# Half blocks of 78 destinations instead of 72, and extra keys added in small chunks between tiles, in a gather and scatter-add kernel

## The chip, the core and the metric

The kernel runs on one core of a Trainium2 chip. The metric is the device time of one execution in microseconds (us), the median of several runs. Engine names are those of the profile: PE is TensorE (matmul), PEld its weight loads, DVE is VectorE, ACT is ScalarE, POOL is GpSimd, SP is SyncE.

## The reference

The task is one GraphSAGE layer with mean aggregation. 800,000 edges go between 12,500 nodes, with random source and destination, and each node has 64 features.

```python
N, deg, D = 12500, 64, 64
E = N * deg
src = randint(0, N, E);  dst = randint(0, N, E)

def reference(x, src, dst, deg_inv, w_self, w_neigh):
    N = x.shape[0]
    nsum = _segment_sum(x[src], dst, N)
    h_neigh = nsum * deg_inv[:, None]
    return x @ w_self + h_neigh @ w_neigh
```

So for each edge a row of x is fetched by source and added into a sum by destination. The two small products and the scaling follow at the end.

## The kernel before

**Buckets.** Sources are cut into 98 blocks (NB) of 128. Destinations are cut into blocks of two halves with HN = 72 destinations each, which gives 87 destination blocks (NDB). A pair of a destination block and a source block is a bucket: 87 x 98 = 8526 buckets (NBID). Each bucket has 128 slots for edges, 64 (H) for each half of its destinations. An edge is one 32-bit key that holds destination block, source block, half, source and destination in it. Buckets are stored as rows of keys: part 0 has 128 rows of 41 buckets each, part 1 has 128 rows of 27 (KPRS).

**First half of the time.** `make_keys` builds the keys. `sort_runs` sorts the 6250 keys of each partition on DVE (lines 230 to 245). `find_rows` counts where each row starts in each of the 128 sorted runs, `gather_runs` (L473, POOL, one indirect DMA per run) brings the pieces of all runs to the partition of their row, and `merge_runs` (L284, L296, L313, L328, DVE) merges them. The lengths that a merge keeps at each level are LENS. `find_buckets` (part 0, on ACT, L610) counts where each bucket's middle lies in its row; `gather_buckets` (L633, POOL) fetches a window of 2 x SIDE = 2 x (64 + EXT) keys around each middle; `decode_buckets` splits the windows, four buckets at a time (L680 to L685 on DVE, L690 and L694 on ACT, a transpose on PE at L700, a copy on ACT at L701), into the 64 + 64 slots and writes the slots' sources to memory (sl). Part 1 goes the same way later, with `find_and_gather` counting on DVE (L612).

**Extra keys.** A half of a bucket with more than 64 edges has keys left over. They lie in the EXT keys at either end of the window. `beyond` (L717, L720) makes them stand out as positive numbers, `pieces` (L745) takes the 8 largest of each of PCS = 8 interleaved pieces of a row, and `leftovers` compacts them: the rows go to memory and come back 16 rows (GRP) to a partition (L756, L757), the 8 largest of 16 pieces are taken again, and the result goes to memory (lt) and back to turn it. This gives 8 chunks per part, each of at most 128 extra keys from 16 rows. `wide` is a row of numbers that the place of a key within its destinations is compared with.

**Second half of the time.** `nodes` walks the buckets in tiles of 8. For each tile `one_hots` has loaded the slots' sources (slb, SP) and built on DVE two one-hot matrices per 28 buckets: ohs (L799, 128 x 3584, which source) and ohd (L802, 128 x 28 x 72, which destination). `gather` multiplies ohs with the block of x on PE (L827, one matmul of 128 columns per bucket) into PSUM (ct), and ACT (L837), or from tile SHARE = 540 on in some tiles DVE (L835), copies the result to xg. `sums` multiplies xg with ohd into acc (L883, two matmuls of 72 columns per bucket, one for each half of the slots, which use 64 rows of the array each). OCT = 7 destination blocks make an octet; its sums stand in two PSUM tiles. When an octet is done, the extra keys of all its chunks are added: their rows of x were fetched (L864, POOL, from 300 buckets ahead on), one-hot matrices of 504 columns are built (L876, DVE), and matmuls of 504 columns add them (L888). Then g is copied out (L891, L893), and `finish` multiplies with the weights (L951), scales (L957), adds (L958) and writes (L959, issued on POOL).

**What runs beside the tiles.** `sums_and_merge` drives everything of part 1 from the loop over tiles: for each tile it grants the merge of part 1 a budget of 280 ns (`t += 280`); when that merge has ended it makes one step of `find_and_gather` in every second tile, then one step of `decode_buckets` per tile, and then `leftovers(1)`. Part 1 must be decoded before its first bucket is due. A scheduler that works on a modelled time orders the instructions of each engine, except where a manual schedule is given (the sort and the first merges).

Of the kernel before, what the change touches and what calls it, by code (L numbers as in the profile page):

```python
# [46 lines left out]
CHK = 128 // GRP  # L47
BIGBITS = 0x7E000000
# [10 lines left out]
BEHIND = 6  # L59
NEARLY = 36  # L60
LAG = 4
OCT = 7

# [276 lines left out]
class Kernel:  # L340
    def __init__(self, tc, ctx, ins, outs):
        self.tc, self.nc, self.ctx = tc, tc.nc, ctx
        self.I, self.O = ins, outs
        self.keep = ctx.enter_context(tc.tile_pool(name="keep", bufs=1))
        self.dram = ctx.enter_context(tc.tile_pool(name="dram", bufs=1, space=DRAM))
        self.d1 = self.dram.tile([128, PITCH1], F32, name="d1")
        self.sl = self.dram.tile([NCOL, 128], BF, name="sl")
        self.xt = self.dram.tile([NB * 128, 128], FH, name="xt")
        self.tops = [self.dram.tile([128, PCS * 9], F32, name=f"tops{p}") for p in range(2)]
        self.lt = [self.dram.tile([CHK, 128], F32, name=f"lt{p}") for p in range(2)]  # L350
        self.d2 = [self.dram.tile([128, PITCH2[p]], F32, name=f"d2_{p}") for p in range(2)]

    def setup(self):
# [15 lines left out]
        for p in range(2):  # L369
# [6 lines left out]
                       allow_small_or_imprecise_dtypes=True)  # L376
        self.wide = keep.tile([128, OCT * HN], FH, name="wide")
        nc.gpsimd.iota(self.wide, pattern=[[1, OCT * HN]], base=0, channel_multiplier=0,
                       allow_small_or_imprecise_dtypes=True)
# [287 lines left out]
    def decode_buckets(self, part, v, vp, mps):  # L667
# [56 lines left out]
        for step in range(per * (len(groups) - 1) + plan[0][0] + 1):  # L724
            for wait, what in plan:
                g, odd = divmod(step - wait, per)
                if not odd and 0 <= g < len(groups):
                    held[g] = what(*groups[g], held.get(g))
            yield min(step // 2 * 4, kpr - 1)
            if part == 0 and step == per * (NEARLY // 4 - 1):  # L730
                beyond(0, NEARLY, 0, PCS - 2)()
                yield -1
        if part == 0:
            beyond(NEARLY, kpr - NEARLY, PCS - 2, 2)()
        else:
            pick = beyond(0, kpr, 0, PCS)
            yield kpr
            pick()
# [7 lines left out]

    def leftovers(self, part):


        nc = self.nc  # L750
        pool = self.fin
        n = PCS * 9 + 1
        nc.scalar.dma_start(self.tops[part], self.top.rearrange("p j i -> p (j i)"))
        yield 3
        many = pool.tile([CHK, GRP, n], F32, name="many")
        nc.vector.memset(many, 0.0)  # L756
        nc.scalar.dma_start(many[:, :, :PCS * 9], self.tops[part].rearrange("(a b) i -> a b i", b=GRP))  # L757
        yield 8
        top = pool.tile([CHK, GRP, 8], F32, name="ltop")
        self.pieces(many.rearrange("p b i -> p (b i)"), GRP * n, top, GRP)  # L760
        nc.vector.tensor_scalar(many.rearrange("p b i -> p (b i)")[:, :128].rearrange("a (j i) -> a j i", i=8), top, 0.0, None,
                                op0=OP.is_gt, op1=OP.add,
                                accum_out=self.cnt[:CHK, sum(NCNT) + 1 + part:sum(NCNT) + 2 + part])
# [7 lines left out]
        t = pool.tile([128, CHK], I32, name="lt")  # L771
        s = pool.tile([128, CHK], I32, name=f"ls{part}")
# [4 lines left out]
        q = pool.tile([128, CHK], I32, name="lq")  # L777
# [3 lines left out]
        nc.vector.tensor_scalar(t, k, 1, 0x2000, op0=OP.logical_shift_right, op1=OP.bitwise_and)  # L781
        nc.vector.tensor_tensor(q, q, t, op=OP.add)
        z = pool.tile([128, CHK], F32, name="lz")
        nc.vector.tensor_scalar(z, k.bitcast(F32), 0.0, 32768.0, op0=OP.is_equal, op1=OP.mult)
        place = pool.tile([128, CHK], F32, name=f"lp{part}")
        nc.vector.tensor_tensor(place, z, q, op=OP.add)
# [18 lines left out]
    def nodes(self, pool, aps, mps):  # L805
# [7 lines left out]
        done = []  # L813
        acc = ohl = lx = own = None

# [24 lines left out]
        def chunks(o):  # L840

            lo, hi = o * OCT * NB, min((o + 1) * OCT * NB, NBID)
            return [(p, c) for p in range(2) for c in range(CHK)
                    if BASE[p] + (c + 1) * GRP * KPRS[p] > lo and BASE[p] + c * GRP * KPRS[p] < hi]

        def sums(job):

            nonlocal acc, ohl, lx
            b0, xg, cols = job
# [5 lines left out]
            if b0 % (OCT * NB) == 0:  # L855
                acc = [aps.tile([128, OCT * HN], F32, name=f"acc{h}", bufs=1) for h in range(2)]
            if b0 % (OCT * NB) == 0:
                lx = []
            if b0 + LEAD >= end and len(lx) < len(chunks(o)) and b0 // 8 % 3 == 0:
                p, c = chunks(o)[len(lx)]  # L860
                ix = pool.tile([128, 1], I32, name="lxi", bufs=6)
                nc.vector.tensor_copy(ix, self.left[p][1][:, c:c + 1])  # L862
                x = pool.tile([128, 128], FH, name="lx", bufs=4)
                nc.gpsimd.indirect_dma_start(  # L864
                    out=x, out_offset=None, in_=self.xt,
                    in_offset=bass.IndirectOffsetOnAxis(ap=ix.bitcast(U32), axis=0))
                lx.append(x)
                self.picked = len(done)
            if b0 + 64 >= end and ohl is None:
                ohl = []  # L870
                assert len(lx) == len(chunks(o))
                for (p, c), x in zip(chunks(o), lx):
                    m = pool.tile([128, 2, OCT * HN], FH, name="ohl", bufs=4)
                    place = self.left[p][0]
                    for h in range(2):
                        nc.vector.tensor_scalar(m[:, h, :width], self.wide[:, :width], place[:, c:c + 1],  # L876
                                                -float(o * OCT * HN + h * 8192), op0=OP.subtract, op1=OP.is_equal)
                    ohl.append((m, x))
            for i, d in enumerate(cols):
                db, sb = divmod(b0 + i, NB)  # L880
                for h in range(2):
                    r = slice(h * H, (h + 1) * H)
                    nc.tensor.matmul(acc[h][:, db % OCT * HN:(db % OCT + 1) * HN], xg[r, i * 128:(i + 1) * 128], d[r],  # L883
                                     start=db % OCT == 0 and sb == 0, stop=False)
            if last:
                for i, (m, x) in enumerate(ohl):
                    for h in range(2):
                        nc.tensor.matmul(acc[h][:, :width], x, m[:, h, :width], start=False, stop=i == len(ohl) - 1)  # L888
                ohl = None
                g = self.fin.tile([128, OCT, 2, HN], F32, name="g", bufs=1)  # L890
# [194 lines left out]
    def sums_and_merge(self, es, mps, aps, u, l2, l2b, l2a, counts):  # L1085
# [31 lines left out]
        self.picked = -9  # L1117
        left, left_at = self.leftovers(0), 2
        t = 0
        for n in self.nodes(fin, aps, mps):  # L1120
# [8 lines left out]
            if merge:  # L1129
                t += 280  # L1130
                while merge and t > 0:
# [10 lines left out]
            elif find:  # L1142
                if n % 2 == 0 and self.picked < n - 1 and next(find, None) is None:
                    find = None
                    decode = self.decode_buckets(1, self.v, vp, mps)
            elif decode:
                if next(decode, None) is None:
                    assert n < 128 * KPRS[0] // 8 - 12
                    decode = None
                    left, left_at = self.leftovers(1), 0  # L1150
        vb.close()
# [28 lines left out]
```

## Time and profile before

| | |
|---|---|
| runs | 2134.72, 2136.84, 2137.42 us; median 2136.84 |
| span of the profiled execution | 2141.8 us (the profile gives no other time for it) |
| busy share of the span | DVE 93%, ACT 59%, PE 48%, PE weight loads 41%, POOL 28% |
| chain that ended last, by engine | PE 36%, DVE 30%, POOL 19%, issue 8%, ACT 5%, DMA 2% |
| mean granted TensorE clock | 0.774 of full speed, 0.98 while the tiles run |

The span falls into five stages, and the busy shares above are averages over all of them. From 0 to 512 us DVE sorts. From 512 to 1056 us POOL gathers pieces and DVE merges them. From 1056 to 1561 us tiles run and DVE merges part 1 beside them. From 1561 to 1685 us tiles run and DVE finds and decodes the buckets of part 1. From 1685 to 2132 us only tiles run. A tile is counted by its 8 matmuls of L827.

### The profile page before, as it was taken

What the parts mean: (1) busy time and instruction counts of PE and PEld (TensorE: products, weight loads), DVE (VectorE), ACT (ScalarE), POOL (GpSimd) and SP (SyncE); (2) the same over time, 40 slices, a digit from 0 to 9 for tenths busy, and PEclk for the clock granted to TensorE, in tenths of its full rate; (3) what the DMA queues carried; (4) which work ended last, traced back from release to release, by engine and by line L of the source; (5) the groups of instructions that cost most, each with busy time, mean ns of one, the idle gap of its engine ahead of it and who ended that gap; (6) DMA issues with size and microseconds to landing.
All of it is one profiled execution on the core that took longest, in us unless ns stands there. A gap on an engine that the chain in (4) does not pass through costs nothing.

```text
span 2141.8 us, 59532 instructions
## 1 busy us (share of the span) xinstructions
PE 1022.8 (48%) x26057; PEld 885.4 (41%) x26057; DVE 1998.3 (93%) x2172; ACT 1260.8 (59%) x1744; POOL 593.8 (28%) x867
## 2 busy tenths in 40 slices
PE   0140000000000000000299999999987799999997
PEld 0130000000000000000188788787876687888886
DVE  8999999999899999999999999999999988898887
ACT  7470000009700000162399999999998788888886
POOL 1000000000889888879810100000143000000000
PEclk9995555555555555555599999999999899999999
DMA  6040000000010000012477777777886677877874
GB/s 191 14 111 0 0 0 0 0 24 37 21 23 20 19 15 12 13 58 70 150 263 279 279 280 270 272 281 269 285 295 243 222 283 284 296 289 275 280 297 157
DMA packets 108220, 330.78 MB, mean 154 GB/s; under 512 B 53680, under 2 KB 61824, under 8 KB 107440
## 3 DMA queue, kind: packets, MB, share of 16 engines
q1 hardware_dynamic: 90784, 306.65, 39.4%
q0 software_dynamic: 14352, 18.65, 4.1%
q8 instruction: 205, 3.36, 0.6%
q10 hardware_dynamic: 2816, 1.61, 0.3%
q14 instruction: 63, 0.52, 0.1%
HBM read 307.86 MB, written 18.99 MB: 153 GB/s over the span
## 4 chain that ended last, share of the span: by engine, by line
PE 36%; DVE 30%; POOL 19%; issue 8%; ACT 5%; DMA 2%; ACTq 0%; DVEq 0%; POOLq 0%; SPq 0%
PE ct L827 21%; PE acc L883 14%; POOL u L473 13%; DVE a L232 10%; DVE b L232 10%; POOL pad L384 3%; ACT xg L837 2%; DVE ohd L802 2%; POOL v L633 2%; DVE ohs L799 2%; PE po L951 1%; DVE xg L835 1%; ACT junk L610 1%; DVE u L296 1%; ACT junka L454 1%
## 5 line engine op out<-in xcount | busy, mean ns | idle before, releaser
L837 ACT ACTIVATE xg<-ct 128x1024 f16<-128x1024 f32 (+1 forms) x991 | 934.8, 1105 | 102.2 <-PE ct L827 83.7
L827 PE MATMUL ct<-xh,ohs 128*128 128x128 f16 x8526 | 606.8, 223 | 47.7 <-issue 19.9
L827 PEld LDWEIGHTS <-ohs 128*128 128x128 f16 x8526 | 501.9, 99 | 91.7 <-issue 38.0
L473 POOL DMA_INDIRECT u<-d,ix x256 | 327.6, 1280 | 532.6 <-ACT junka L454 491.3
L296 DVE TENSOR_TENSOR u<-u 128x256 f32<-128x256 f32 (+47 forms) x494 | 452.6, 947 | 22.4 <-ACT u L280 15.3
L883 PE MATMUL acc<-ohd,xg 64*128 64x72 f16 x17052 | 413.0, 195 | 49.5 <-issue 27.1
L799 DVE TENSOR_SCALAR ohs<-slb,pidx 128x3584 f16<-128x3584 bf16 x305 | 351.0, 1151 | 32.8 <-PE ct L827 28.4
L883 PEld LDWEIGHTS <-xg 64*128 64x128 f16 x17052 | 327.1, 95 | 128.2 <-issue 47.4
L802 DVE TENSOR_TENSOR ohd<-iota,dlT 128x2016 f16<-128x2016 bf16 x305 | 366.7, 1202 | 0.0
L700 PE MATMUL tr<-idb,l 128*128 128x128 bf16 x68 | 9.1, 275 | 464.2 <-ACT l L694 460.6
L232 DVE TENSOR_TENSOR a<-b 128x106 f32<-128x106 f32 (+31 forms) x114 | 228.6, 2058 | 1.3
L232 DVE TENSOR_TENSOR b<-a 128x106 f32<-128x106 f32 (+36 forms) x112 | 227.4, 2081 | 1.0
L280 ACT ACTIVATE u<-u 128x256 f32<-128x256 f32 (+15 forms) x94 | 47.4, 595 | 281.6 <-DVE u L284 281.6
L463 PE MATMUL stp<-idf,st 128*128 128x128 f32 x2 | 0.9, 446 | 422.3 <-DVE st L461 422.3
L700 PEld LDWEIGHTS <-l 128*128 128x128 bf16 x68 | 5.5, 117 | 467.5 <-ACT l L694 464.0
L959 POOL DMA_DIRECT2D out<-o x24 | 22.8, 952 | 574.2 <-DVE o L958 491.2
L463 PEld LDWEIGHTS stp<-idf,st 128*128 128x128 f32 x2 | 0.4, 182 | 422.7 <-issue 422.7
L235 ACT ACTIVATE a<-b 128x106 f32<-128x106 f32 (+12 forms) x20 | 13.5, 709 | 214.1 <-DVE b L232 207.6
L835 DVE CAST xg<-ct 128x1024 f16<-128x1024 f32 x78 | 95.2, 1222 | 43.3 <-PE ct L827 43.2
L864 POOL DMA_INDIRECT lx<-xt,lxi x28 | 52.5, 1876 | 292.2 <-DVE lxi L862 165.9
L633 POOL DMA_INDIRECT v<-d,ix x68 | 89.9, 1323 | 63.5 <-ACT ix L663 44.6
L235 ACT ACTIVATE b<-a 128x1024 f32<-128x1024 f32 (+19 forms) x32 | 23.0, 771 | 130.4 <-DVE a L232 130.2
(135 smaller groups left out, 888.4 us busy)
## 6 DMA issues: line engine op xcount, KB each, us to landing
slb<-sl SPq DMA_DIRECT2D x305, 896.0 KB
u<-d,ix POOLq DMA_INDIRECT x256, 2.5
xt<-xh SPq DMA_DIRECT2D x1, 3136.0 KB
own<-os SPq DMA_DIRECT2D x12, 256.0 KB
fo<-own SPq DMA_DIRECT2D x24, 126.0 KB
out<-o POOLq DMA_DIRECT2D x24, 126.0 KB, 4.3
rd<-dst SPq DMA_DIRECT2D x4, 521.0 KB
rs<-src SPq DMA_DIRECT2D x4, 521.0 KB
```

What stands on the lines that cost most here:

```text
L232: nc.vector.tensor_tensor(view(dst, lo + sh, [[st, g], [1, l]]), x, y, op=op)
L296: nc.vector.tensor_tensor(to, at(cur, ln + lo, n), at(cur, lo + k, n), op=op)
L384: self.nc.gpsimd.memset(self.pad, 0.0)
L473: nc.gpsimd.indirect_dma_start(out=u[:nr, p * w:(p + 1) * w], out_offset=None, in_=src, in_offset=bass.IndirectOffsetOnAxis(ap=self.start[ ...
L633: self.nc.gpsimd.indirect_dma_start(out=self.v[:, k].bitcast(F32), out_offset=None, in_=flat(self.d2[part], 128 * PITCH2[part]), in_offset ...
L799: nc.vector.tensor_scalar(s.rearrange("p c s -> p (c s)"), b, self.pidx[:, :1], None, op0=OP.is_equal)
L802: nc.vector.tensor_tensor(d, self.iota[:, None].to_broadcast([128, 14, HN, 2]), ix, op=OP.is_equal)
L827: nc.tensor.matmul(ct[:, i * 128:(i + 1) * 128], cols[i][0], self.xh[:, (b0 + i) % NB].rearrange("p a f -> p (a f)"), start=True, stop=True)
L835: nc.vector.tensor_copy(xg[:, :cnt * 128], ct[:, :cnt * 128])
L837: nc.scalar.activation(xg[:, :cnt * 128], ct[:, :cnt * 128], AF.Copy)
L864: nc.gpsimd.indirect_dma_start(out=x, out_offset=None, in_=self.xt, in_offset=bass.IndirectOffsetOnAxis(ap=ix.bitcast(U32), axis=0))
L883: nc.tensor.matmul(acc[h][:, db % OCT * HN:(db % OCT + 1) * HN], xg[r, i * 128:(i + 1) * 128], d[r], start=db % OCT == 0 and sb == 0, stop ...
```

## The change

The halves of a destination block get 78 destinations, so there are 81 destination blocks, 81 x 98 = 7938 buckets, rows of 38 and 25 buckets, octets of 6 blocks and groups of 117 destinations in `finish`. The slots of a half stay 64, so more keys are left over: the windows get 31 extra keys at either end, PCS becomes 17, and the leftovers are compacted to chunks of 2 rows (part 0) or 3 rows (part 1), which are 64 and 43 chunks. Such a chunk spans at most 76 buckets, so its keys belong to at most two destination blocks. Its one-hot matrix has 4 x 78 = 312 columns (`pick`), and `add` adds it with two matmuls of 78 or 156 columns in the place where its last bucket has been passed, between two tiles; it is picked 64 buckets (LEAD) ahead. A chunk that reaches over the end of an octet is picked once for each side; there are 118 picks. The indices for the fetch are read from their tile in place, and the turn through memory (lt) becomes a transpose on PE. The budget of the merge beside the tiles goes from 280 to 315 ns, and the finding of part 1 makes steps in two tiles of three instead of one of two.

```diff
-HN = 72
+HN = 78
-FB = 126
+FB = 117
-KPRS = (41, 27)
+KPRS = (38, 25)
-LENS = ((64, 108, 188, 336, 608, 1144, 2176, 4208),
-        (48, 80, 132, 236, 420, 780, 1472, 2824))
+LENS = ((64, 108, 190, 340, 612, 1152, 2196, 4248),
+        (48, 80, 132, 236, 422, 786, 1484, 2848))
-LEAD = 300
-EXT = 25
+LEAD = 64
+EXT = 31
-PCS = 8
-GRP = 16
-CHK = 128 // GRP
+PCS = 17
+GRP = (2, 3)
+CHK = [-(-128 // g) for g in GRP]
-NEARLY = 36
+NEARLY = 32
-OCT = 7
+OCT = 6
...
-        nc.scalar.dma_start(self.lt[part].rearrange("a (j i) -> a j i", i=8), top)
-        yield 3
-        k = pool.tile([128, CHK], I32, name="lk")
-        src = self.lt[part]
-        nc.scalar.dma_start(k.bitcast(F32), bass.AP(tensor=src.tensor, offset=src.offset, ap=[[1, 128], [128, CHK]]))
-        yield 8
+        ps = mps.tile([128, chk], F32, name="ltp", tag="ct", bufs=3)
+        nc.tensor.transpose(ps, top.rearrange("a j i -> a (j i)"), self.idf[:chk, :chk])
+        k = pool.tile([128, chk], I32, name="lk")
+        nc.vector.tensor_copy(k.bitcast(F32), ps)
+        yield 1
...
+        def pick(p, c, first):
+
+            x = pool.tile([128, 128], FH, name="lx", bufs=4)
+            nc.gpsimd.indirect_dma_start(
+                out=x, out_offset=None, in_=self.xt,
+                in_offset=bass.IndirectOffsetOnAxis(ap=self.left[p][1][:, c:c + 1].bitcast(U32), axis=0))
+            m = pool.tile([128, 4 * HN], FH, name="ohl", bufs=4)
+            nc.vector.tensor_scalar(m, self.wide, self.left[p][0][:, c:c + 1], -float(first * HN),
+                                    op0=OP.subtract, op1=OP.is_equal)
+            self.picked = len(done)
+            return x, m
+
+        def add(x, m, first, lo, hi):
+            for h in range(2):
+                at = (2 * h + lo - first) * HN
+                nc.tensor.matmul(acc[h][:, lo % OCT * HN:(hi % OCT + 1) * HN], x, m[:, at:at + (hi + 1 - lo) * HN],
+                                 start=False, stop=False, skip_group_check=True)
...
-            if b0 + LEAD >= end and len(lx) < len(chunks(o)) and b0 // 8 % 3 == 0:
-                p, c = chunks(o)[len(lx)]
-                ix = pool.tile([128, 1], I32, name="lxi", bufs=6)
-                nc.vector.tensor_copy(ix, self.left[p][1][:, c:c + 1])
-                x = pool.tile([128, 128], FH, name="lx", bufs=4)
-                nc.gpsimd.indirect_dma_start(
...
-            if b0 + 64 >= end and ohl is None:
...
-                    for h in range(2):
-                        nc.vector.tensor_scalar(m[:, h, :width], self.wide[:, :width], place[:, c:c + 1],
-                                                -float(o * OCT * HN + h * 8192), op0=OP.subtract, op1=OP.is_equal)
-                    ohl.append((m, x))
+            while got and got[0][0] <= b0:
+                add(*got.pop(0)[1:])
+            while due and len(got) < 3 and due[0][1] in self.left and (due[0][0] <= b0 + LEAD):
+                e, p, c, first, lo, hi = due.pop(0)
+                got.append((e, *pick(p, c, first), first, lo, hi))
...
             if last:
-                for i, (m, x) in enumerate(ohl):
-                    for h in range(2):
-                        nc.tensor.matmul(acc[h][:, :width], x, m[:, h, :width], start=False, stop=i == len(ohl) - 1)
-                ohl = None
+                for use in got:
+                    add(*use[1:])
+                assert not due
...
-                t += 280
+                t += 315
...
-                if n % 2 == 0 and self.picked < n - 1 and next(find, None) is None:
+                if n % 3 and self.picked < n - 1 and next(find, None) is None:
```

More of the change, by code (lines that the diff above doesn't have):

```diff
@@ L376, in setup @@
                        allow_small_or_imprecise_dtypes=True)
-        self.wide = keep.tile([128, OCT * HN], FH, name="wide")
-        nc.gpsimd.iota(self.wide, pattern=[[1, OCT * HN]], base=0, channel_multiplier=0,
+        self.wide = keep.tile([128, 4 * HN], FH, name="wide")
+        nc.gpsimd.iota(self.wide, pattern=[[1, 4 * HN]], base=0, channel_multiplier=0,
                        allow_small_or_imprecise_dtypes=True)
@@ L745, in pieces, with leftovers @@
             self.nc.vector.max(out=top[:, j, :8], in_=view(f, j, [[pcs, len(range(j, n, pcs))]]))
-    def leftovers(self, part):
+    def leftovers(self, part, mps):
         nc = self.nc
         pool = self.fin
-        n = PCS * 9 + 1
+        n = PCS * 9
+        grp, chk = GRP[part], CHK[part]
+        whole, rest = divmod(128, grp)
         nc.scalar.dma_start(self.tops[part], self.top.rearrange("p j i -> p (j i)"))
         yield 3
-        many = pool.tile([CHK, GRP, n], F32, name="many")
-        nc.vector.memset(many, 0.0)
-        nc.scalar.dma_start(many[:, :, :PCS * 9], self.tops[part].rearrange("(a b) i -> a b i", b=GRP))
+        many = pool.tile([chk, grp, n], F32, name="many")
+        if rest:
+            nc.vector.memset(many, 0.0)
+        nc.scalar.dma_start(many[:whole], self.tops[part][:whole * grp].rearrange("(a b) i -> a b i", b=grp))
+        if rest:
+            nc.scalar.dma_start(many[whole:, :rest], self.tops[part][whole * grp:].unsqueeze(0))
@@ L780, in leftovers @@
         nc.vector.scalar_tensor_tensor(q, t, float(HN), q, op0=OP.mult, op1=OP.add)
-        nc.vector.tensor_scalar(t, k, 1, 0x2000, op0=OP.logical_shift_right, op1=OP.bitwise_and)
-        nc.vector.tensor_tensor(q, q, t, op=OP.add)
-        z = pool.tile([128, CHK], F32, name="lz")
+        nc.vector.tensor_scalar(t, k, 14, 1, op0=OP.logical_shift_right, op1=OP.bitwise_and)
+        nc.vector.scalar_tensor_tensor(q, t, float(2 * HN), q, op0=OP.mult, op1=OP.add)
+        z = pool.tile([128, chk], F32, name="lz")
         nc.vector.tensor_scalar(z, k.bitcast(F32), 0.0, 32768.0, op0=OP.is_equal, op1=OP.mult)
-        place = pool.tile([128, CHK], F32, name=f"lp{part}")
+        place = pool.tile([128, chk], F32, name=f"lp{part}")
         nc.vector.tensor_tensor(place, z, q, op=OP.add)
@@ L813, in nodes @@
         done = []
-        acc = ohl = lx = own = None
+        acc = due = got = own = None
         turn = 0
@@ L842, in chunks @@
             lo, hi = o * OCT * NB, min((o + 1) * OCT * NB, NBID)
-            return [(p, c) for p in range(2) for c in range(CHK)
-                    if BASE[p] + (c + 1) * GRP * KPRS[p] > lo and BASE[p] + c * GRP * KPRS[p] < hi]
+            out = []
+            for p in range(2):
+                per = GRP[p] * KPRS[p]
+                for c in range(CHK[p]):
+                    b = BASE[p] + c * per
+                    a, e = max(b, lo), min(b + per, hi, BASE[p] + 128 * KPRS[p])
+                    if a < e:
+                        out.append((e, p, c, b // NB, a // NB, (e - 1) // NB))
+            return out
+        def pick(p, c, first):
[13 more added lines that the diff above has]
+                                 start=False, stop=False, skip_group_check=True)
         def sums(job):
-            nonlocal acc, ohl, lx
+            nonlocal acc, due, got
             b0, xg, cols = job
@@ L856, in sums @@
                 acc = [aps.tile([128, OCT * HN], F32, name=f"acc{h}", bufs=1) for h in range(2)]
[L857 to L878 removed]
+                due, got = chunks(o), []
+            while got and got[0][0] <= b0:
[3 more added lines that the diff above has]
+                got.append((e, *pick(p, c, first), first, lo, hi))
             for i, d in enumerate(cols):
@@ L1117, in sums_and_merge @@
         self.picked = -9
[L1118 removed]
+        left, left_at = self.leftovers(0, mps), 2
         t = 0
```

24 lines of the change are left out of this document (12 added, 12 removed).

## The prediction

> **What bounds the kernel now.** I read the page first, then the busy time by stage, and last the order of time inside each stage. The page's costliest groups:
>
> ```profile
> L837 ACT ACTIVATE xg<-ct 128x1024 f16<-128x1024 f32 (+1 forms) x991 | 934.8, 1105 | 102.2 <-PE ct L827 83.7
> L827 PE MATMUL ct<-xh,ohs 128*128 128x128 f16 x8526 | 606.8, 223 | 47.7 <-issue 19.9
> L799 DVE TENSOR_SCALAR ohs<-slb,pidx 128x3584 f16<-128x3584 bf16 x305 | 351.0, 1151 | 32.8 <-PE ct L827 28.4
> L883 PE MATMUL acc<-ohd,xg 64*128 64x72 f16 x17052 | 413.0, 195 | 49.5 <-issue 27.1
> L802 DVE TENSOR_TENSOR ohd<-iota,dlT 128x2016 f16<-128x2016 bf16 x305 | 366.7, 1202 | 0.0
> ```
>
> These five scale with the number of buckets, on three engines at once. The windows by stage show which engine limits where (columns: stretch, its length, then busy us and instructions of PE, PEld, DVE, ACT, POOL; then granted clock and DMA):
>
> ```profile
> 512.00:1056.00 544.00, 7.26 (x43) 3.91 (x43) 505.98 (x778) 149.04 (x409) 457.10 (x738) 0.50 0.12 33
> 1056.00:1561.00 505.00, 472.60 (x12241) 407.97 (x12242) 477.71 (x510) 484.38 (x547) 52.86 (x39) 0.98 0.78 278
> 1561.00:1632.00 71.00, 59.67 (x1502) 50.34 (x1499) 67.04 (x98) 59.77 (x88) 36.33 (x29) 0.95 0.80 282
> 1632.00:1685.00 53.00, 38.68 (x901) 33.16 (x898) 51.94 (x82) 42.02 (x54) 8.34 (x9) 0.89 0.59 213
> 1685.00:2132.00 447.00, 412.03 (x11218) 362.88 (x11215) 392.25 (x432) 381.25 (x412) 32.17 (x26) 0.98 0.76 274
> ```
>
> and the same stretches for L827 alone (PE, PEld) give the tiles, eight matmuls each:
>
> ```profile
> 1056.00:1561.00 505.00, 292.03 (x4065) 240.92 (x4066) 0.98 0.78 278
> 1561.00:1632.00 71.00, 35.13 (x494) 29.01 (x491) 0.95 0.80 282
> 1632.00:1685.00 53.00, 24.04 (x298) 19.48 (x295) 0.89 0.59 213
> 1685.00:2132.00 447.00, 255.63 (x3680) 212.48 (x3677) 0.98 0.76 274
> ```
>
> Stage A, tiles and merge (1056 to 1561): 508 tiles, 0.994 us each; ACT is busy 96%, DVE 95%, PE 94%. Stage F, finding (to 1632): 62 tiles at 1.15 us, DVE 94% busy. Stage D, decoding (to 1685): 37 tiles at 1.42 us, DVE 98%. Stage B, tiles alone: 460 tiles at 0.972 us, with PE at 92%, DVE 88% and ACT 85%; no engine is full, they wait for each other. So where DVE has side work, DVE decides; where it has none, the cost of a tile does.
>
> **The change, part by part.** *Tiles.* 8526 buckets become 7938, 1065.75 tiles become 992.25. A tile's work on ACT stays. On PE it grows: columns of L883 go from 72 to 78. In full flow PE shows
>
> ```profile
> 2122.00 1.07 PE L827 MATMUL ct<-xh,ohs 128*128 128x128 f16 x16
> 2123.00 0.70 PE L883 MATMUL acc<-ohd,xg 64*128 64x72 f16 x32
> 2123.63 1.07 PE L827 MATMUL ct<-xh,ohs 128*128 128x128 f16 x16
> ```
>
> 16 matmuls of 128 columns take 1.00 us from start to start, 62.5 ns each, and 16 pairs of 72 columns 0.63 us, 39.4 ns a pair. The slope is 23.1 / 56 = 0.41 ns a column, so a pair grows by 2.5 ns and a tile by 0.020 us. Ends: nothing, or in proportion (39.4 x 6 / 72 = 3.3 ns a pair, 0.026 us a tile).
>
> The Trainium skill ("TensorE: Matmul & The Clock Gate", section "Wait — 56ns, not 53.3ns?") says that matmuls never start less than about 25 ns apart however few columns they have. By that rule the six columns might cost nothing and the sum below would be some 8 us lower; the row does not agree with it, since 32 matmuls in 0.63 us are 19.7 ns apart.
>
> *One-hots on DVE.* Between starts:
>
> ```profile
> 1137.27 1.15 DVE L799 TENSOR_SCALAR ohs<-slb,pidx 128x3584 f16<-128x3584 bf16 x1
> 1138.33 1.21 DVE L802 TENSOR_TENSOR ohd<-iota,dlT 128x2016 f16<-128x2016 bf16 x1
> 1139.45 1.13 DVE L876 TENSOR_SCALAR ohl<-wide,lp 128x504 f16<-128x504 f16 x4
> ```
>
> L799 takes 1.06 us, L802 1.12 us. L802 gets 2184 elements, at most 1.12 x 8.3% = 0.09 us more. So 28 buckets cost 2.27 us, not 2.18, in 284 rounds, not 305.
>
> *Picks and adds.* 56 L876 of 504 columns (0.28 us each) become 118 of 312 columns; between 0.28 us (overhead alone) and 0.17 us (columns alone) I take 0.23: 27 us against 16, of which 54 picks fall in stage A (+6.5 us of DVE), the rest spread. 28 copies of indices (L862) go. The adding matmuls:
>
> ```profile
> L888 PE MATMUL acc<-ohl,lx 128*128 128x504 f16 x52 | 14.0, 397 | 0.0
> ```
>
> 0.27 us each for 504 columns; by the slope the new 236, 121 columns on average, cost about 60 ns, 14 us in all. PE gains and loses nothing there, and the bursts at the end of an octet are spread.
>
> *Merge.* LENS grow by 0.6%, and two steps less of the first decode (below) leave about 5 us of merge to the tiles: +6 us of DVE in stage A. The budget of 315 ns shortens the stage in tiles: in the order of DVE the first count of part 1 stands behind 137 rounds of one-hots, before behind 147. Stage A on DVE: 477.7 - 10 x 2.18 + 137 x 0.09 + 6.5 + 6 + 1.6 (two more `finish`) - 4 (copies, first compaction) = 478 us, the same, but for 137 x 3.5 less the 6.4 tiles that PE is behind = 473 tiles. That is 1.01 us of DVE a tile, over ACT's 0.95, so DVE is the bound: at 97.5% busy (between the 94% and 98% of F and D) 491 us, 14 less. Ends: 478 (never idle) and 505 (as now).
>
> *Finding.* Here the change costs. With 81 blocks the last has 20 destinations, not 116, and the windows over which part 1 counts must take in all rows: 25 counts over 34,328 elements instead of 27 over 16,184 (from the program's own table).
>
> ```profile
> 1559.55 0.33 DVE L612 TENSOR_SCALAR_CACHE_REDUCE junk<-u,c 128x110 bf16<-128x110 f32 x1
> ...
> 1620.78 1.22 DVE L612 TENSOR_SCALAR_CACHE_REDUCE junk<-u,c 128x976 bf16<-128x976 f32 x1
> 1621.93 0.08 DVE L612 DVE_READ_ACCUMULATOR junk<-u,c 128x1 f32 x1
> 1622.05 1.24 DVE L612 TENSOR_SCALAR_CACHE_REDUCE junk<-u,c 128x986 bf16<-128x986 f32 x1
> 1623.21 0.08 DVE L612 DVE_READ_ACCUMULATOR junk<-u,c 128x1 f32 x1
> ```
>
> From 110 to 986 elements the duration grows by 0.91 us, 1.04 ns an element. From start to start the first of a pair takes 1.27 us, the second 1.16 (what follows starts beside its read of the accumulator), so 0.19 us stand beside the elements: 35.7 + 25 x 0.19 = 40 us, against 22. Stage F: 16 rounds x 2.27 + 40 + 2 = 78, with 2% idle 80 us (now 71). Stage D: 12 rounds (27) + six and a quarter groups of split (2.27 us each, 15) + the extra keys of 25 x 62 elements (7.4, with 17 L745 for 8) + five copies of ct (5.7) + 2.6 = 57 us (now 53). F and D together +13 us, between 8 and 22.
>
> *First half.* Three windows less for POOL (L633), one group of four less in the decode:
>
> ```profile
> 1010.00 0.69 DVE L680 TENSOR_TENSOR v<-v,c 128x512 int32<-128x512 int32 x1
> 1017.33 0.69 DVE L680 TENSOR_TENSOR v<-v,c 128x512 int32<-128x512 int32 x1
> 1025.86 0.68 DVE L680 TENSOR_TENSOR v<-v,c 128x512 int32<-128x512 int32 x1
> ```
>
> A group takes 7.9 us; with two counts on ACT less (about 2 us), 1.3 us more for L745 and 1.5 us longer merges that is -7 us, between -4 and -11. The sort stays.
>
> *Stage B.* DVE's order ends the decode after 165 rounds; PE, 5.5 tiles behind, is at 572, so 420 tiles remain (now 460). A tile costs 0.972 + 0.020 (PE) + 0.005 (DVE has 0.03 us more, at 88% busy) = 0.997 us: 419 us, -28. Ends: 408 (pace as now) and 433 (0.026 us for the columns, DVE's 0.033 in full).
>
> The sum: -7 - 14 + 13 - 28 = -36 us. The profiled execution spans 2141.8 us, 5 above the median of the runs; I take the difference over: 2136.8 - 36 = 2101 us.
>
> **Rivals.** (1) *Everything overlaps better*: DVE never idles in A and B keeps its pace: 13 and 11 us more, 2077. For it: PE's full flow above is 1.63 us for two tiles, far under the pace. Against: no stage with side work on DVE reaches 100%. (2) *DVE takes the gain*: A keeps its 505 us, B comes to 433: 2129. For it: DVE was 95% busy in A and gets no less work there. (3) *Slower, because adds wait for their rows.* A pick stands 8 tiles ahead, 7.8 us; the fetch takes
>
> ```profile
> L864 POOL DMA_INDIRECT lx<-xt,lxi x28 | 52.5, 1876 | 292.2 <-DVE lxi L862 165.9 <-PE ct L827 121.3 <-issue 3.6
> lx<-xt,lxi POOLq DMA_INDIRECT x27, 6.5
> POOL out L959 <- DVE o L958: 491.2, 21, 45.2
> ```
>
> 1.9 + 6.5 = 8.4 us. PE stands in order behind an add, and everything behind PE. It decides from 36 / 118 = 0.31 us a pick on; if each pick is issued only at its place, each is 0.6 us late, 71 us, 2172. For it: POOL does stand up to 45 us behind an `out` that waits for DVE (third row). Against: a pick now waits only for the add four before it, so POOL runs up to three chunks (28 tiles) ahead except behind an `out`. (4) *Switching the array.* L883 uses 64 rows, an add 128. In PE's order 55 adds stand between two runs of L883, two switches more each; a switch costs at most one matmul's own 223 ns, so 24 us, with 10 in B where PE counts: 2111. In the rows above the switch cannot be told from the flow.
>
> The Trainium skill ("TensorEngine Tiling (Array Packing)", section "Key Properties") says that a change of tiling mode drains the engine. That is rival (4), and speaks against adds between tiles; the trace before shows no number for it.
>
> **How the numbers follow.** Forecast 0.55, its own range 2083 to 2122 (half of each term's distance to its ends); rival (1) 0.15, (2) 0.12, (3) 0.12, (4) 0.06. The predicted time is the forecast's. The range leaves out half of (1), and (3): 2074 to 2136. A measurement of this kernel tells 0.2%, 4.3 us, from no change. Slower is (3) without its mild cases, and a little of (2): 0.12. Same is what (2) and a mild (3) leave near 2137: 0.06. Faster: 0.82.
>
> **What would show it.** L827 x7938 and ACT's L837 at about 870 us; tiles starting near 1049; the first count of part 1 about 491 us later with DVE over 95%; the counts of part 1 (L612) at about 41 us busy and the stages F and D near 137 us; then 0.997 us a tile. Wrong would be: PE waits of some us for the new fetch or one-hot in front of an add; a first count of part 1 not earlier than 1555; a pace over 1.03 us in the last stage.

## The result, and the profile after

The changed kernel takes 2150.8 us in the median of 9 runs (2141.9 to 2166.2), the kernel before on the same chip 2135.4 us. The ratio is 1.0083, with a 95% interval of 1.0055 to 1.0112: slower by 18 us by the ratio, where 36 us less were forecast. The profiled execution took 2148.23 us, with a span of 2146.5 us. The experiments ran on three chips, each run beside the kernel before on its own chip (medians 2140.6, 2135.5 and 2148.2 us), so runs are compared by their ratios to it. Below, a ratio is turned into us by 2135.4, and paces are us per tile of eight buckets.

The page's groups of the changed kernel (line, engine, operation, tiles, count; then busy us, mean ns of one; then idle time ahead and who ended it):

```profile
L840 ACT ACTIVATE xg<-ct 128x1024 f16<-128x1024 f32 x931 | 879.1, 1058 | 170.9 <-PE ct L830 159.0
L830 PE MATMUL ct<-xh,ohs 128*128 128x128 f16 x7938 | 562.0, 225 | 53.6 <-DVE ohs L802 21.8
L895 PE MATMUL acc<-ohd,xg 64*128 64x78 f16 x15876 | 420.1, 201 | 65.0 <-issue 31.0
L805 DVE TENSOR_TENSOR ohd<-iota,dlT 128x2184 f16<-128x2184 bf16 x284 | 366.1, 1289 | 0.0
L859 POOL DMA_INDIRECT lx<-xt,ls x118 | 199.4, 1690 | 302.7 <-PE acc L871 266.7
```

The work on buckets fell as the change says: L830 has 7938 matmuls, ACT's copies fell from 935 to 879 us. But ACT now stands 159 us waiting for PE, not 84, and POOL issues 118 fetches (L859), where there were 28. The groups of the new work, from the view by lines:

```profile
L871 PE MATMUL acc<-ohl,lx 128*128 128x156 f16 (+1 forms) x236 | 33.2, 224 | 18.8 <-DMA lx<-xt,ls 18.8
L863 DVE TENSOR_SCALAR ohl<-wide,lp 128x312 f16<-128x312 f16 x118 | 35.0, 297 | 0.0
L611 DVE TENSOR_SCALAR_CACHE_REDUCE junk<-u,c 128x126 bf16<-128x126 f32 (+24 forms) x25 | 41.0, 1640 | 0.4
```

The adds (L871) stand 18.8 us waiting for the rows that they add. The busy time by stage (A tiles and merge, F finding, D decoding, B tiles alone), and the same for L830 alone:

```profile
1053.00:1556.00 503.00, 454.64 (x11543) 400.43 (x11543) 479.30 (x525) 458.36 (x523) 126.85 (x84) 0.96 0.79 264
1556.00:1627.00 71.00, 47.77 (x1104) 41.28 (x1102) 70.60 (x79) 47.04 (x70) 31.86 (x28) 0.82 0.69 231
1627.00:1681.00 54.00, 45.83 (x1113) 39.07 (x1111) 52.36 (x82) 49.64 (x67) 22.08 (x21) 0.98 0.72 237
1681.00:2136.00 455.00, 407.07 (x10509) 361.01 (x10511) 384.67 (x436) 356.83 (x387) 91.87 (x60) 0.96 0.76 254
...
1053.00:1556.00 503.00, 268.94 (x3800) 225.38 (x3800) 0.96 0.79 264
1681.00:2136.00 455.00, 238.98 (x3422) 200.87 (x3422) 0.96 0.76 254
```

Stage A makes 475 tiles at 1.059 us (before 508 at 0.994) in the time that it took before; DVE has 479 us of work in it, as forecast, and idles 24. Stage B makes 428 tiles at 1.064 us (before 0.972). The gain in tiles is given back in both by the pace, and no engine is fuller for it: in B, DVE is busy 85% and PE 89%.

What a loss looks like in B, from the timeline (start, duration, engine, line, and in brackets the idle time ahead):

```profile
1768.98 0.47 PE L895 MATMUL acc<-ohd,xg 64*128 64x78 f16 x16
1769.32 1.78 POOL L859 DMA_INDIRECT lx<-xt,ls  x1 [6.93 <-PE acc L871]
1769.39 0.28 PE L830 MATMUL ct<-xh,ohs 128*128 128x128 f16 x2
1772.37 1.65 PE L830 MATMUL ct<-xh,ohs 128*128 128x128 f16 x14 [2.70 <-issue]
1773.96 1.22 PE L895 MATMUL acc<-ohd,xg 64*128 64x78 f16 x32
```

PE stops two matmuls into a tile for 2.7 us, waiting for nothing that the profile shows ("issue"), while POOL issues a fetch, and then runs slower for a while: 14 matmuls of L830 in 1.59 us, 114 ns each (62.5 in full flow before), and 1.22 us for sums that take 0.77 elsewhere. The granted clock is 0.5 from 1772.3 to 1775.7 us. In B it stood at 0.5 nine times, 34 us in all; in B of the kernel before it was four times and 17 us.

### The profile page after: what moved, and what is told of

Same layout as the page of the kernel before. It is cut to its first block, busy times and chain, and to the rows that moved or that the text cites. A ratio compares the mean times of both kernels' runs of the same rounds, so it can differ in the third digit from the quotient of the medians.

```text
span 2146.5 us, 56332 instructions
## 1 busy us (share of the span) xinstructions
PE 1001.1 (47%) x24484; PEld 877.9 (41%) x24484; DVE 1992.9 (93%) x2165; ACT 1197.8 (56%) x1677; POOL 732.5 (34%) x951
## 4 chain that ended last, share of the span: by engine, by line
DVE 31%; PE 24%; POOL 20%; issue 16%; ACT 4%; DMA 3%; DVEq 0%; SPq 0%; POOLq 0%; ACTq 0%
POOL u L472 14%; PE ct L830 13%; DVE a L232 10%; DVE b L232 10%; PE acc L895 10%; POOL pad L383 4%; DVE ohd L805 3%; DMA lx<-xt,ls 3%; DVE ohs L802 2%; POOL v L632 1%; DVE u L296 1%; DVE junk L611 1%; ACT xg L840 1%; POOL lx L859 1%; ACT junk L609 1%
## 5 line engine op out<-in xcount | busy, mean ns | idle before, releaser
L840 ACT ACTIVATE xg<-ct 128x1024 f16<-128x1024 f32 x931 | 879.1, 1058 | 170.9 <-PE ct L830 159.0
L830 PE MATMUL ct<-xh,ohs 128*128 128x128 f16 x7938 | 562.0, 225 | 53.6 <-DVE ohs L802 21.8
L830 PEld LDWEIGHTS <-ohs 128*128 128x128 f16 x7938 | 471.0, 101 | 91.8 <-issue 35.7
L296 DVE TENSOR_TENSOR u<-u 128x256 f32<-128x256 f32 (+48 forms) x494 | 455.5, 952 | 23.9 <-ACT u L280 16.6
L895 PE MATMUL acc<-ohd,xg 64*128 64x78 f16 x15876 | 420.1, 201 | 65.0 <-issue 31.0
L895 PEld LDWEIGHTS <-xg 64*128 64x128 f16 x15876 | 337.6, 97 | 133.0 <-issue 62.1
L805 DVE TENSOR_TENSOR ohd<-iota,dlT 128x2184 f16<-128x2184 bf16 x284 | 366.1, 1289 | 0.0
L802 DVE TENSOR_SCALAR ohs<-slb,pidx 128x3584 f16<-128x3584 bf16 x284 | 326.3, 1149 | 32.1 <-PE ct L830 30.0
L859 POOL DMA_INDIRECT lx<-xt,ls x118 | 199.4, 1690 | 302.7 <-PE acc L871 266.7
L838 DVE CAST xg<-ct 128x1024 f16<-128x1024 f32 x68 | 82.9, 1219 | 59.2 <-PE ct L830 59.0
L632 POOL DMA_INDIRECT v<-d,ix x63 | 78.6, 1247 | 56.5 <-ACT ix L662 36.5
```

The source lines that it names most:

```text
L296: nc.vector.tensor_tensor(to, at(cur, ln + lo, n), at(cur, lo + k, n), op=op)
L632: self.nc.gpsimd.indirect_dma_start(out=self.v[:, k].bitcast(F32), out_offset=None, in_=flat(self.d2[part], 128 * PITCH2[part]), in_offset ...
L802: nc.vector.tensor_scalar(s.rearrange("p c s -> p (c s)"), b, self.pidx[:, :1], None, op0=OP.is_equal)
L805: nc.vector.tensor_tensor(d, self.iota[:, None].to_broadcast([128, 14, HN, 2]), ix, op=OP.is_equal)
L830: nc.tensor.matmul(ct[:, i * 128:(i + 1) * 128], cols[i][0], self.xh[:, (b0 + i) % NB].rearrange("p a f -> p (a f)"), start=True, stop=True)
L838: nc.vector.tensor_copy(xg[:, :cnt * 128], ct[:, :cnt * 128])
```

## The experiments

Read by itself, that trace suggested two culprits on PE: the adds between the tiles (theory 1), and a pair of 78 columns that takes 5 ns more, not 2.5 (theory 2). The first four runs were made to tell these apart, with DVE as the third.

**No adds.**

```diff
-                add(*got.pop(0)[1:])
+                got.pop(0)
...
-                for use in got:
-                    add(*use[1:])
```

> The changed kernel with its 107 chunks picked as now (the fetch on POOL, the mask on DVE), but without the 236 matmuls that add them; so the extra keys are left out of the output. Theory 1, the adds: each add between two tiles costs TensorE two changes between 64-row and 128-row matmuls, some with a wait for the fetched rows, about 0.14 us at a tile's edge and 0.34 us inside a tile's sums, some 44 us in all against 11 us before; without them 2150 - 30 to 40 = 2110 to 2120 us. Theory 2, the columns: a pair of 78 columns takes 5 ns longer than one of 72, twice the forecast, and the adds hide beside it; 2140 to 2150 us. Theory 3, DVE (the masks, the wide find windows): the stage with the merge stays at 500 us, since DVE is busy 479 us of it, and only the last one gains, 2150 - 14 = 2136 us.

Measured: 1.0032 (1.0005 to 1.0060), 2152.1 us beside 2140.6. Against the changed kernel's 1.0083 that is 11 us less, uncertain by 8; theory 1 wanted 30 to 40. Stage B stays at 1.08 us a tile without a single add. Theory 1 falls as the main cause.

**Six columns fewer to multiply.**

```diff
-   nc.tensor.matmul(acc[h][:, db % OCT * HN:(db % OCT + 1) * HN], xg[r, i * 128:(i + 1) * 128], d[r],
+   w = HN if sb == 0 else 72
+   nc.tensor.matmul(acc[h][:, db % OCT * HN:db % OCT * HN + w], xg[r, i * 128:(i + 1) * 128], d[r][:, :w],
```

> The changed kernel, in which the pair matmuls multiply 72 of the 78 columns (all 78 only for the first source block of each destination block), so that six columns of each half block are left out of the output; the count of tiles, the masks, the adds and all of DVE's work stay. Theory 2 (5 ns for each of 7938 pairs): 2150 - 30 to 40 = 2110 to 2120 us. The forecast's price of 2.5 ns: 2130 us or above. Theory 1 (adds) and theory 3 (DVE), if the columns are hidden: 2145 to 2150 us.

Measured: 1.0053 (1.0025 to 1.0081), 6 us below the changed kernel and uncertain by 9. Theory 2 as the main cause falls too.

**Adds held back to the start of a pair of tiles.**

```diff
-            while got and got[0][0] <= b0:
+            while got and got[0][0] <= b0 and b0 % (OCT * NB) % 16 == 0:
```

> The changed kernel with each add held back until the next sums that begin a pair of tiles, so that it lies where TensorE changes from counting to summing anyway, not between two tiles' sums. Theory 1 (adds, by the changes they force inside the sums): 55 or so adds cost 0.14 instead of 0.34 us, and their rows have up to 1 us more to arrive; 2150 - 11 to 18 = 2132 to 2139 us. Theory 1b (adds, by the waits for the fetched rows alone): a few us, 2143 to 2148. Theory 2 and theory 3: 2150 us, no change.

Measured: 1.0055 (1.0031 to 1.0080), 6 us less than the changed kernel and uncertain by 8: where the adds lie does not decide.

**The new chunks alone, with half blocks of 72.** All sizes as before (HN, FB, KPRS, LENS, EXT, PCS, NEARLY, OCT), with the new `pick`, `add` and `leftovers`, and chunks of 2 or 3 rows.

> One half of the change alone: the half blocks, lists and windows of before (72 destinations, 41 and 27 buckets in a row, 25 extra places), with the new chunks of 2 or 3 rows (107 of them, fetched, masked and added between the tiles). Theory 1 (adds cost 33 us more than those of before): 2135 + 25 to 35 = 2160 to 2170 us. Theory 2 (columns and nothing else): 2135 to 2140 us. Theory 3, in so far as it is the masks on DVE (107 x 0.3 us against 48 x 2 old ones, 19 us more, of which the part under the merge counts): 2140 to 2150 us.

Measured: 1.0307 (1.0271 to 1.0344), 66 us slower than before, twice what theory 1 named, and 48 us slower than the whole change. So the half blocks of 78 gain much, the new chunk machinery costs more than that, and neither its matmuls nor the columns are the main reason. What was left of the machinery: the fetches on POOL and the masks on DVE. Two counts fitted the fetches (theory 4): an unexplained stop of PE comes beside one, as above, and L859 has 118 instead of 28. The next runs took the machinery apart.

**No fetches, no masks, no adds.** `pick` returns nothing, the adds go as above.

> The changed kernel without the new work between the tiles: no fetch of the chunks' rows, no masks, no adds, so that the extra keys are left out of the output; columns, lists, windows and the planning stay. Theory 4 (the fetches: an indirect DMA for each chunk delays the other transfers, TensorE's instructions among them, and TensorE then stands and runs on at the lower clock): the last stage falls from 1.07 to 1.01 us a tile (0.90 at full clock with 78 columns, and the excess of 0.11 that before had), 26 us, and with the masks gone from DVE the stage with the merge by 16 us; 2150 - 35 to 45 = 2105 to 2115 us. Theory 5, that the wider half block itself slows the tiles (its columns, its wider one-hots): 2150 - 15 at most, 2135 to 2150 us.

**Masks and adds, but no fetches.**

```diff
-            x = pool.tile([128, 128], FH, name="lx", bufs=4)
-            nc.gpsimd.indirect_dma_start(
-                out=x, out_offset=None, in_=self.xt,
-                in_offset=bass.IndirectOffsetOnAxis(ap=self.left[p][1][:, c:c + 1].bitcast(U32), axis=0))
+            x = self.xh[:, 0].rearrange("p a f -> p (a f)")
```

> The changed kernel with its masks and its 236 adds, but without the fetches: every add multiplies rows that lie in SBUF anyway, so that the extra keys' part of the output is left wrong. Theory 4 (fetches): the last stage falls to 1.01 to 1.03 us a tile, 2150 - 20 to 30 = 2120 to 2130 us, and most of what the kernel without fetches, masks and adds gains is gained here. Theory 6 (the masks: 0.3 us of DVE between the one-hots, 107 times): no more than 5 us, 2145 to 2150 us.

Measured: 0.9736 (0.9717 to 0.9755) for the bare kernel, 2078.4 us, and 0.9795 (0.9775 to 0.9814) with masks and adds back, 2092.6 us. Masks and adds together cost 13 us (uncertain by 6); the 118 fetches, with the waits for them, cost 61 us (1.0083 less 0.9795, uncertain by 7), 0.52 us each. Both kernels are further down than theory 4 named, since stage A gains nearly as much as B. Stages A and B of the kernel without fetches, all engines and L830 (here too) alone:

```profile
1053.00:1533.00 480.00, 452.68 (x11605) 399.65 (x11605) 477.23 (x521) 458.44 (x525) 21.30 (x25) 0.97 0.74 272
1648.00:2085.00 437.00, 406.15 (x10704) 360.19 (x10705) 395.10 (x454) 363.64 (x397) 12.11 (x13) 0.98 0.72 267
...
1053.00:1533.00 480.00, 267.56 (x3816) 223.87 (x3814) 0.97 0.74 272
1648.00:2085.00 437.00, 239.27 (x3494) 200.34 (x3493) 0.98 0.72 267
```

DVE has the same 477 us of work in A, but idles 3 us instead of 24, and B runs at 1.001 us a tile.

**The kernel before with 78 fetches more.** In `sums`, from the 65th call on, every 13th:

```diff
+            if nsum > 60 and nsum % 13 == 0:
+                x = pool.tile([128, 128], FH, name="lxd", bufs=2)
+                nc.gpsimd.indirect_dma_start(
+                    out=x, out_offset=None, in_=self.xt,
+                    in_offset=bass.IndirectOffsetOnAxis(ap=self.left[0][1][:, :1].bitcast(U32), axis=0))
```

> The kernel before with some 70 more fetches of 128 rows of 256 bytes between its tiles (every 13th tile), into a tile that nobody reads; nothing else is changed. Theory 4: the last stage goes from 0.985 to 1.03 to 1.07 us a tile, TensorE's idle time that nothing in the profile explains grows from 25 to some 38 us there; 2137 + 25 to 45 = 2162 to 2182 us. Without theory 4: 2137 to 2142 us.

Measured: 1.0137 (1.0114 to 1.0159), 29 us or 0.37 us a fetch. B runs at 1.02 us a tile, a little under the 1.03 to 1.07 named:

```profile
1671.00:2153.00 482.00, 266.70 (x3780) 222.16 (x3780) 0.96 0.75 265
```

A cost of the same kind appears where nothing else of the change is there, and nobody reads what is fetched. PE's unexplained idle time, though, did not grow to 38 us there as expected, only to 29.

**Chunks of 4 rows.** `GRP = (4, 4)`, masks of 6 x 78 columns, three blocks instead of two, three buffers for the masks.

> The changed kernel with chunks of 4 rows in both parts, 64 instead of 107, each added to at most three blocks (masks of 468 instead of 312 columns). Theory 4: 118 fetches become some 75, near the 48 or so of before, and three fifths of what the fetches cost come back; 2150 - 12 to 20 = 2130 to 2138 us. Theory 5 and 6: 2145 to 2150 us.

Measured: 0.9961 (0.9941 to 0.9981), 2126.1 us, with 76 fetches: 26 us below the changed kernel and faster than before, somewhat better than named. The masks and adds are fewer too, and a fetch brings more keys, so this run alone doesn't price the fetches.

Why a fetch of 32 KB costs half a microsecond, when each tile's one-hots bring in eight times as much, was open. The fetches cost 0.52 us each in the changed kernel, 0.37 us where 78 of them read the first chunk of the kernel before. Counting the drawn edges gives a reason: a chunk of the changed kernel holds some 18 keys in its 128 places, one of the kernel before 34 or 16 (49 in the first, which the 78 fetches read), one of the kernel with new chunks and 72 destinations 4 or 3. Every empty place has index 0, so most of a fetch's 128 reads go to one and the same row of `xt` (theory 7). In my reading of the trace's transfer records, a fetch's pieces of eight rows took 0.62 us in the median between 1690 and 2050 us, 1.64 us at the ninth decile and up to 3 us; the 7168-byte pieces of `slb` took 0.27.

**Empty places spread over rows.**

```diff
+        w = pool.tile([128, chk], F32, name="lw")
+        nc.vector.tensor_scalar(w, k.bitcast(F32), 0.0, self.pidx[:, :1], op0=OP.is_equal, op1=OP.mult)
+        nc.vector.scalar_tensor_tensor(s, w, 98.0, s, op0=OP.mult, op1=OP.add)
```

> The changed kernel, whose chunks fetch for each of their empty places a row of its own (98 times the partition's number) instead of row 0; a chunk has about 19 keys in 128 places, so some 109 of 128 reads of a fetch go to one row now. The masks are zero there, so the output is the same. Theory 7 (the reads of one row stand behind each other, and the transfers of the DMA engines behind them): packets of the fetches, 0.6 to 0.7 us in the median now, come near those of 0.15 us, and most of the fetches' 58 us come back: 2105 to 2125 us. Theory 4 in its first form (each fetch costs 0.5 us, whatever it reads): 2145 to 2152 us.

Measured: 0.9923 (0.9896 to 0.9949), 2130.9 us beside 2148.2: the same 118 fetches of the same size, 34 us less than the changed kernel (uncertain by 8). By the ratio to 2135.4 that is 2119 us, inside the 2105 to 2125 that theory 7 named; of what the fetches cost it is little more than half. The pieces' median fell from 0.62 to 0.084 us. The DMA queues in 1690 to 2050 us (packets, MB, share of the 16 engines), first of the changed kernel, then with spread places:

```profile
q0 software_dynamic: 1785, 2.33, 9.4%
q8 instruction: 65, 1.06, 1.1%
```

```profile
q0 software_dynamic: 2016, 2.61, 3.7%
```

More bytes in well under half the time. What remains of the fetches' 61 us is 27, and one row of this kernel has 25 us of idle time that may be the most of it, adds that wait for their rows:

```profile
L874 PE MATMUL acc<-ohl,lx 128*128 128x156 f16 (+1 forms) x236 | 33.0, 223 | 25.4 <-DMA lx<-xt,ls 25.4
```

**The kernel before, spread.** The same three lines in its `leftovers`.

> The kernel before with the empty places of its 28 chunk fetches spread over rows of their own, and nothing else. Theory 7: 28 fetches at 0.3 to 0.45 us, 2136 - 8 to 13 = 2123 to 2128 us. Theory 4 in its first form: 2134 to 2138 us.

Measured: 0.9974 (0.9949 to 1.0000): 6 us less, a little short of the 8 to 13 named and only just told from nothing.

**The kernel before with 78 plain transfers.** As above, with consecutive rows instead of indices:

```diff
-                nc.gpsimd.indirect_dma_start(
-                    out=x, out_offset=None, in_=self.xt,
-                    in_offset=bass.IndirectOffsetOnAxis(ap=self.left[0][1][:, :1].bitcast(U32), axis=0))
+                nc.gpsimd.dma_start(x, self.xt[128 * (nsum % NB):128 * (nsum % NB) + 128])
```

> The kernel before with the same 78 additional transfers of 128 rows of 256 bytes on POOL's queue, but plain ones, of 128 rows that lie one behind the other, into a tile that nobody reads. Theory 7: such transfers cost next to nothing, 2136 to 2142 us, against the 29 us of the fetches. Theory 4b (anything that goes through POOL's queue between the tiles delays the others): 2155 to 2165 us.

Measured: 1.0020 (0.9992 to 1.0048): 4 us, not told from nothing, against 29 for as many fetches of as many bytes on the same queue. Queue q0 between 1690 and 2050 us in the kernel before, with 78 fetches more, and with 78 plain transfers more:

```profile
q0 software_dynamic: 960, 1.62, 3.0%
```

```profile
q0 software_dynamic: 1728, 2.35, 5.5%
```

```profile
q0 software_dynamic: 1760, 2.38, 4.0%
```

Theory 7 holds for 34 of the 61 us: these are the reads of one row. That the fetches are indirect may add something that these runs don't separate.

**All that helps.** Chunks of 4 rows, spread places, and `LEAD = 160`, so that a pick may stand 20 tiles ahead.

> The kernel with chunks of 4 rows, with the empty places spread as in the other run, and picks that may stand 20 instead of 8 tiles ahead, so that the waits of adds for their rows (7 us in the last stage) go. Theory 7: 2085 to 2105 us. Theory 4 in its first form: 2126 - 7 = 2119 us.

Measured: 0.9793 (0.9763 to 0.9824), 2100.9 us beside 2148.2: 44 us faster than the kernel before by the ratio, as theory 7 named, and the fastest of those that leave nothing out. Three edits work together here, and their shares are not told apart. Its rows for A and B, L830 alone, and its adds:

```profile
1053.00:1531.00 478.00, 266.80 (x3800) 223.01 (x3800) 0.98 0.78 276
1645.00:2084.00 439.00, 243.37 (x3522) 203.58 (x3522) 0.98 0.76 270
```

```profile
L874 PE MATMUL acc<-ohl,lx 128*128 128x156 f16 (+2 forms) x152 | 22.8, 233 | 3.3 <-DMA lx<-xt,ls 3.3
```

B runs at 0.997 us a tile, and the waits of the adds are down to 3.3 us.

## Why the prediction was wrong, step by step

The failed step is "Picks and adds". It priced the masks on DVE (0.23 us each; they took 0.30) and the adds on PE ("PE gains and loses nothing there"; with the masks they cost 13 us in all), and it gave the 90 additional fetches no term: they appear only in rival (3), as a time that an add may have to wait for. All 118 fetches cost 61 us, 0.52 us each; at that price the 90 additional ones are 47 us, an estimate. Of the 61 us, 34 went when the empty places got rows of their own, and most of the rest is probably adds that waited. The other terms were about right in sum: without any fetch the kernel takes 0.9795 of before, 44 us less, and with the 28 old fetches kept at 0.52 us each it would be some 29 less (an estimate), on either side of the 36 that were forecast. The range's upper end, 2136 us, stops short of the 2172 of rival (3), and the time lies 15 us above it.

The terms, measured from event to event in the profiled executions; that of the changed kernel spans only 5 us more than that of the kernel before, where the ratio of the runs says 18, so a term may be some us off:

| Term | Forecast | Changed kernel | Without fetches |
|---|---|---|---|
| start of the tiles | -7 | -3 | -3 |
| A, to the first count of part 1 | -14 | -1 | -23 |
| F and D, to the last split of the decode | +13 | +9 | +9 |
| B | -28 | 0 | -29 |
| sum, the end of the kernel among it | -36 | +5 | -47 |

- *Tiles.* 473 were forecast for A and 420 for B, at the forecast's bounds; 475 and 428 came. The order of DVE's work told these counts well.
- *Stage A.* DVE's work was 479 us (forecast 478). The share of time that it is busy was taken as 97.5%, from stages of the kernel before; it is 95.3% with the fetches and 99.4% without. So the 24 us of idle time went with the fetches, and the share was not one of DVE's own work.
- *F and D.* The counts over wider windows came as forecast (41 us and 2 us of reads of the accumulator, for 40). The two stages took 125 us by the forecast's bounds (114 by those of the table, which end at the last split), 12 less than forecast, of which some 5 us are that 90 tiles came to lie in them, not 98 (8 tiles at 2.27 us for 3.5 of them on DVE); for the rest no row stands out.
- *Columns.* 2.5 ns a pair was too little as PE's own price:

```profile
1711.67 0.77 PE L895 MATMUL acc<-ohd,xg 64*128 64x78 f16 x32
1712.38 1.07 PE L830 MATMUL ct<-xh,ohs 128*128 128x128 f16 x16
1713.38 0.77 PE L895 MATMUL acc<-ohd,xg 64*128 64x78 f16 x32
```

16 pairs take 0.71 us from start to start (0.63 before), 44.4 ns a pair: 5 ns more, also outside both named ends (0 and 3.3). But the pace that was built on it, 0.997 us, is met by the kernel without fetches (1.001) and by the last one (0.997), and taking the six columns away gained 6 us, uncertain by 9. The mis-sized price did not decide.
- *Rival (3)*, slower because the adds wait for their rows, had the sign. Its mechanism is there: 18.8 us of waits, 25.4 where the reads were spread. It had counted on 71 us of it, and the larger part of the loss was of another kind. By its waits alone (18.8 us for 118 picks, 0.16 us each) its turning point of 0.31 us a pick was not reached; with all that a fetch cost, 0.52, it was. So its sign came true in part by luck.
- *Rival (4)*, switching the array: holding the adds back to a tile's edge gained 6 us, uncertain by 8. It is not the main cause, and a price for a switch is not shown.
- *Rival (1)*, better overlap: its condition, that DVE idles next to nothing in A, is met where the fetches are gone (99.4%), though its text held that no stage gets there.
- *Rival (2)* described the shape of A (503 us, DVE 95% busy with no less work than before). But nearly the same work, 477 us, took 480 us without the fetches, so it was the fetches that kept A long. B at 455 us is longer than its 433.

What would show it wrong was named, and all three signs came: waits for the fetch ahead of an add (10 of them, up to 5.4 us), the first count of part 1 at 1555.4, a pace of 1.064 in B.

One link stays open: how slow reads on queue q0 reach PE. Between 1690 and 2050 us PE's unexplained idle time in L830 and L895 is 21 us in the changed kernel and 5.6 with spread places, and its granted clock in B 0.96 against 0.98. In my reading of the trace's records, 14 of the 23 gaps of over 0.4 us in that stretch (24 of 40 us) end 1.15 to 1.65 us after a 16 KB instruction load on q8 has landed, where chance would put a tenth; with spread places it is 9 gaps and 6 us. The stop shown above ends 1.2 us after such a load. Late instruction loads would fit these two kernels. But counted in the same way the kernel before has 21 such gaps and 25 us, with 78 fetches more 23 and 27 us, and with 78 plain transfers more 25 and 31 us, at the least cost. So these gaps do not follow the cost of the fetches, and no run changed the loads alone: how the fetches reach PE stays open. The Trainium skill ("DMA: Bandwidth & Descriptors", section "Queues, rings and completion order") says that each DMA engine goes round the queues that it has work for and finishes a whole packet before it turns to the next. By that rule an instruction load would stand behind a fetch's slow piece; no run here shows the order within one engine.

## What to carry to other kernels

Price every transfer that a change adds by what it does to the transfers beside it, not only by who waits for its data: with the DMA engines three quarters busy, as here, a fetch of 32 KB cost 0.5 us where most of its reads went to one row and some adds waited for it, and a plain transfer of 32 KB some 0.05, not told from nothing. Give the padding entries of an index list rows of their own, not one common row. Finer chunks with fewer keys each were dearer here, not cheaper: they need more fetches, and more of each fetch is padding. How the cost goes with the padding is not shown: the pieces took about 0.6 us in the median both with some 110 and with some 124 empty places of 128. And when a trace shows stops on one engine, take the suspected work away before believing it: here the adds and the columns looked guilty at PE, and taking them away gained 11 us (uncertain by 8) and 6 us (by 9).

## What the runs showed of the hardware that was not expected

An indirect fetch of 128 rows of 256 bytes, of which some 110 are the same row, has pieces of eight rows that take 0.62 us in the median and up to 3 us between 1690 and 2050 us; with distinct rows in the empty places it is 0.084 us in the median, and up to 2 us. 78 such fetches (of a fuller list) cost the kernel before 29 us, 78 plain transfers of the same size 4 us. A pair of 64-row matmuls takes 5 ns longer with 78 columns (44.4 ns) than with 72 (39.4), 0.83 ns a column.
